# Batch 0 of a sketched attention with exact-GELU MLP on one Trainium2 core: 64x64 products against 128x128 products with block-diagonal operands

## The chip, the cores and the metric

The kernel runs on one core of one Trainium2 chip. The metric is the device time in microseconds (us) of one execution; three runs of the kernel before took 259.84, 259.01 and 259.58 us, median 259.58. A core has five engines that run side by side and wait for each other by semaphores: PE (TensorE, matrix products, with its weight loads shown apart as PEld), DVE (VectorE), ACT (ScalarE), POOL (GpSimd) and SP (which here only issues DMAs). Each works through its own instructions in the order of the program.

## The reference

Attention with polynomial-sketch features, and behind it a two-layer MLP. Inputs: q, k, v of shape 4 batches x 4 heads x 1088 tokens x 32, two sketch matrices S1, S2 of 8 x 32, w_in 128 x 2048 and w_out 2048 x 128.

```python
def phi(x):                                  # 64 features of a token
    a = einsum('rd,bhsd->bhsr', S1, x)
    b = einsum('rd,bhsd->bhsr', S2, x)
    return einsum('bhsi,bhsj->bhsij', a, b)  # flattened to 64
kv  = einsum('bhsf,bhsd->bhfd', phi(k), v)
z   = sum(phi(k), over tokens)
num = einsum('bhsf,bhfd->bhsd', phi(q), kv)
den = einsum('bhsf,bhf->bhs', phi(q), z) + 1e-6
x   = num / den                              # heads side by side: 4352 x 128
out = gelu_exact(x @ w_in) @ w_out
```

## The kernel before, in words

Everything is float32. A batch has 1024 main tokens and 64 remaining ones; the main tokens of a batch are two chunks of 512 columns, so there are eight main chunks (n = 0 to 7) and a ninth of all remainders. An added dependency keeps every engine to the order of the program's text.

**Batch 0 starts the kernel** and is built differently from the rest, because the MLP can't begin before its first chunk of x is there. Its steps, in the order of the text:

- Keys are turned on PE (`key_turn` and `key_turn_apart`, lines 341 and 369). `kT[r]` then has on its 128 partitions four consecutive tokens x 32 channels of one head, and 512 columns: two heads (r and r+2) x two chunks x 128.
- `key_products` (L384, its matmul at L390) multiplies them by the sketches. The right operand S12 is 128 x 64 and block-diagonal, four blocks of 32 channels x 16 features. The kernel before uses only the two diagonal halves: for each 64 columns of kT and each half t of the partitions one 64x64 product with 32 columns of S12, 16 instructions for one r. Half t of the partitions goes to bank t.
- `key_features` (L395 on) copies one factor out of PSUM by ACT (L406, or all of it at L403) and multiplies the 64 features on DVE (L407), or for one of the four halves on POOL (L404).
- `expand_products` (L557, query side, chunk 0), then `kv_first` (L434) sums features times values over the tokens. `kv_first` picks the features of token i out of bank t and place as the key products left them.
- The remaining tokens follow (L416, L440), and ACT copies the sums, 2 x 33 columns (32 of kv, one of z) on 2 x 64 partitions, into `kz[0]` (L941).
- `numerators_by_token` (L670): for chunk 0 and 1 the numerators and denominators with the tokens on the partitions. Per token group of 128, per r, per half of 64 tokens and per head pair c one 64x64 product with 33 columns: 8 instructions per group. Chunk 0 goes in two parts of two groups into two banks each; chunk 1 takes four groups at once.
- `expand_products(1)` (L557 again) stands behind chunk 0's numerators on PE.
- `divide` adds 1e-6 to the denominators (L687; for the second part ACT does it, `denominators`, L701), takes the reciprocal (L688) and multiplies (L693), one DVE operation of 128x128 per bank and half.
- The quotients are turned back (L716, L708), copied to xT (L717, L710), and `first_hidden` (L751) and `hidden` (L735) start the MLP; `project` (L872) is its second layer for the first chunks.

Chunk 1's numerators are called at step t == 3 of the MLP loop (L1188), between `hidden` (L735) and `project` (L872). Later batches use other code (L445, L592, L647, L989), and the later MLP blocks a scheme with seven products in place of eight (L821); the change touches neither. At step 40 `repeat_first_z` (L506) takes batch 0's kv and z once more out of `kz[0]` for the remaining tokens.

The PSUM banks come from three rings of two: `hidden_bank` (h_ps), `out_bank` (o_ps) and `work_banks` (w_ps, two banks each).

Of the kernel before, what the change touches and what calls it, by code (L numbers as in the profile page):

```python
# [8 lines left out]
FP = mybir.dt.float32  # L9
U32 = mybir.dt.uint32  # L10
AX = mybir.AluOpType
ACT = mybir.ActivationFunctionType
# [4 lines left out]
def kernel(  # L17
# [18 lines left out]
    pe, dve, act, pool, sp = nc.tensor, nc.vector, nc.scalar, nc.gpsimd, nc.sync  # L36
    B, H, S, D = q.shape
    R = S1.shape[0]
    F = R * R
# [3 lines left out]
    NP = H // 2  # L43
    J = S // 128
    MAIN = J * 128
    REM = S - MAIN
    JC = 4
    CW = JC * 128
    G = 128 // 32
    NCH = J // JC  # L50
    C = D + 1
# [8 lines left out]
    big = ctx.enter_context(tc.tile_pool(name="big", bufs=1))  # L60
# [13 lines left out]
    def halves(banks):  # L74
        return [banks[:, i] for i in range(2)]

    def hidden_bank():
        return hps.tile([128, CW], FP, name="h_ps")

    def out_bank():  # L80
        return ops.tile([128, CW], FP, name="o_ps")
# [149 lines left out]
    kz = [big.tile([128, 128], FP, name=f"kz{b}") for b in range(B)]  # L231

    kz_first = big.tile([128, 128], FP, name="kz_first")

    ones = big.tile([128, D], FP, name="ones")

# [1 line left out]
    pool.memset(v_rem_aug[0], 0.0)  # L238
    pool.memset(v_rem_aug[0][:REM], 1.0)
    dve.memset(ones, 1.0)  # L240

    v_aug = [att.tile([128, NP, J, 2 * D], FP, name="sums") for r in range(2)]
    for t in v_aug:
# [78 lines left out]
    S12 = big.tile([128, H, 2 * R], FP, name="S12")  # L322
# [58 lines left out]
        return dict(out=out, in0=a[:, :, :, None].broadcast_to([128, n, R, R]),  # L381
                    in1=b[:, :, None, :].broadcast_to([128, n, R, R]))

    def key_products(r, banks, col=0):  # L384

        for i in range(2 * NCH):
            for c in range(2):
                for t in range(2):
                    at = i * 128 + c * 64
                    pe.matmul(banks[t][c * 64:(c + 1) * 64, col + i * 32:col + (i + 1) * 32],  # L390
                              lhsT=kT[r][t * 64:(t + 1) * 64, at:at + 64],
                              rhs=S12[t * 64:(t + 1) * 64, 2 * t:2 * t + 2].rearrange("p h r -> p (h r)"),
                              start=True, stop=True)

    def key_features(b, r, banks, by_pool=()):  # L395
        key_products(r, banks)
# [28 lines left out]
    def flat(features):  # L425
        return features.rearrange("p i j -> p (i j)")

    def kv_first(ps, r, tokens=range(J)):

        for i in tokens:  # L430

            ch, t, one = i // 4, i // 2 % 2, i % 2
            for c in range(NP):
                pe.matmul(ps[c * F:(c + 1) * F, r * 2 * D:r * 2 * D + C], lhsT=flat(k_p[0, r][:, t, c * 4 + ch * 2 + one]),  # L434
                          rhs=v_aug[r][:, c, i, :C], start=(r == 0 and i == 0), stop=False, skip_group_check=True)

    def kv_first_rem(ps):
# [67 lines left out]

    def repeat_first_z():  # L506

        of = kz[0].rearrange("f (r x) -> f r x", r=2)
        to = kz_first.rearrange("f (c r d) -> f c r d", c=NP, r=2)
        for c in range(NP):  # L510
            act.copy(out=to[:F, c], in_=of[c * F:(c + 1) * F, :, 0:D])
        zs = att.tile([128, 2, D], FP, name="z_cols")
        pool.tensor_copy(out=zs, in_=of[:, :, D:C].broadcast_to([128, 2, D]))
        held["zs"] = zs

    def turn_first_kv():
# [142 lines left out]

    x_tok = {}  # L660

    def numerators_by_token(n, banks, tokens):

        for at, i in enumerate(tokens):
            for r in range(2):
                for half in range(2):
                    for c in range(NP):
                        rows, col, tok = slice(c * F, (c + 1) * F), (at * 2 + r) * C, i * 128 + half * 64
                        v_at = r * 2 * D
                        pe.matmul(banks[c][half * 64:(half + 1) * 64, col:col + C], lhsT=qp[n][rows, r, tok:tok + 64],  # L670
                                  rhs=kz[0][rows, v_at:v_at + C], start=True, stop=True)

    def x_half(n, i):
        x_tok[n, i] = att.tile([128, 2, H, D], FP, name=f"x_tok{i}", bufs=1)
        return x_tok[n, i]

    def divide(n, banks, tokens, by_head_pair, den=None):

        g = len(tokens) * 2
        given = den is not None  # L680
        if not given:
            den = att.tile([128, NP, JC * 2], FP, name="den_tok")[:, :, :g]
        parts = [slice(c, c + 1) for c in range(NP)] if by_head_pair else [slice(0, NP)]
        nd = [(banks[c.start][:, None] if by_head_pair else banks)[:, :, :g * C].rearrange("p b (g c) -> p b g c", c=C)
              for c in parts]
        for c, x in zip(parts, nd) if not given else ():
            dve.tensor_scalar(out=den[:, c], in0=x[:, :, :, D], scalar1=1e-6, scalar2=None, op0=AX.add)  # L687
        dve.reciprocal(out=den, in_=den)  # L688
        for i in range(len(tokens) // 2):
            to = x_half(n, tokens[0] // 2 + i).rearrange("p j (c r) d -> p c j r d", c=NP)  # L690
            for c, x in zip(parts, nd):
                for b in range(c.stop - c.start):
                    dve.tensor_mul(out=to[:, c.start + b], in0=x[:, b, i * 4:i * 4 + 4, 0:D].rearrange("p (j r) d -> p j r d", r=2),  # L693
                                   in1=den[:, c.start + b, i * 4:i * 4 + 4].rearrange("p (j r) -> p j r", r=2)[:, :, :, None]
                                   .broadcast_to([128, 2, 2, D]))

    def denominators(banks):

        den = att.tile([128, NP, JC * 2], FP, name="den_tok")[:, :, :JC]
        for c, ps in enumerate(banks):  # L700
            act.activation(out=den[:, c], in_=ps[:, :JC * C].rearrange("p (g c) -> p g c", c=C)[:, :, D], func=ACT.Copy, bias=1e-6)  # L701
        return den

    def turn_half_apart(n, i, banks):
# [220 lines left out]
    for i in range(2):  # L925
        query_features(0, i)
    kv_bank = out_bank()
    kv_first(kv_bank, 0, (0, 1, 4, 5))
    key_turn_rem(0, banks[1], by_act)
    kv_first(kv_bank, 0, (2, 3, 6, 7))  # L930
    key_features_rem(0, banks[1])
    kv_first(kv_bank, 1)
    kv_first_rem(kv_bank)
# [3 lines left out]
    w_in[0].exponents()  # L937
    late = []
    query_turn(1, lambda **a: late.append(a))
    kz_of, kv_of = (x.rearrange("f (r x) -> f r x", r=2)[:, :, :C] for x in (kz[0], kv_bank[:, :128]))  # L940
    act.copy(out=kz_of, in_=kv_of)  # L941
    w_in[0].mantissas()
    w_in[0].signs()
    w_in[0].product(pool)
# [3 lines left out]
    by_act(**late[0])  # L948
    w_in[1].low_words()
    parts = [range(2), range(2, JC)]  # L950
    nd = [[hidden_bank(), hidden_bank()], [out_bank(), out_bank()]]
    for banks, tokens in zip(nd, parts):
        numerators_by_token(0, banks, tokens)
    den = denominators(nd[1])
    expand_products(1)
    divide(0, nd[0], parts[0], by_head_pair=True)
    w_in[1].exponent_fields()
    w_in[1].exponents()
    divide(0, nd[1], parts[1], by_head_pair=True, den=den)
    turn_half(0, 0, hidden_bank(), by_act)  # L960
    w_in[1].mantissa_fields()
    turn_half_apart(0, 1, [out_bank(), out_bank()])
# [212 lines left out]
    for t in range(len(steps) + LAG):  # L1175
        if t < 4:

            hidden(0, t)
            if t == 1:
                w_out[0].low_words()  # L1180
                w_out[0].exponents()
                w_out[0].finish()
                w_out[1].fields()
            if t == 2:
                w_out[1].low_words()
            if t == 3:
                banks = work_banks()
                numerators_by_token(1, halves(banks), range(JC))  # L1188
                w_out[1].mantissas(by_pool=True)
                w_out[1].exponents()  # L1190
                divide(1, banks, range(JC), by_head_pair=False)
                w_out[1].signs()
                w_out[1].product()
                project(0, 0)
                project(0, 1, cols=slice(0, 256))
                turn_half(1, 0, work_bank(), by_act)
                project(0, 1, cols=slice(256, 512))
                turn_half(1, 1, work_bank(), by_dve)
            continue
        if t == 4:  # L1200
            first_hidden(1, 0)
            for f, *a in products[t]:
                f(*a)
            first_hidden(1, 1)
        for n in drains[t]:
            drain(n)
        sooner = t == NMAIN * NF
        if sooner:
            for f, *a in products[t]:
                f(*a)  # L1210
        if t < len(steps):
            n, fi = steps[t]
            hidden(n, fi, by_halves=t >= 18 and (n < NMAIN or fi < 5))
        if t < len(steps) and steps[t][0] < NMAIN and steps[t][1] % NB == NB - 1:
            n, b = steps[t][0], steps[t][1] // NB
            if b >= first_block(n):
                token_sums(n, b)
        for f in slots[t]:
            f()
        for n in done[t]:  # L1220
            store(n)
        if t != 4 and not sooner:
            for f, *a in products[t]:
                f(*a)
# [41 lines left out]
```

## Time and profile before

| what | value |
|---|---|
| median of three runs | 259.58 us (259.01 to 259.84) |
| the profiled execution's own time | 259.29 us |
| its span, first to last instruction | 257.5 us (1.8 us lie around it) |
| PE busy | 253.3 us, 98% |
| weight loads (PEld) | 135.0 us, 52% |
| DVE busy | 151.7 us, 59% |
| ACT busy | 114.4 us, 44% |
| POOL busy | 164.1 us, 64% |
| mean granted TensorE clock | 1.0 |

A float32 matrix product appears in the trace as two records, and so does its weight load; a transpose by PE is one record of each. So "x32" beside a group of products means 16 instructions. Shapes such as 64*64 are the rows and columns of the array that the product uses; the shape behind it is that of the moving operand. A record's duration includes the way through the array, so products that follow each other overlap in the list: the pace is read from start to start. A product whose weights are not in yet is recorded early and with a longer duration.

### The profile page before, as it was taken

How to read it: one execution, taken by the hardware profiler on the slowest of the kernel's cores; microseconds unless marked ns; L12 is line 12 of the kernel's file. 1: busy time of each engine (PE TensorE's matmuls, PEld its weight loads, DVE VectorE, ACT ScalarE, POOL GpSimd, SP SyncE). 2: the span in 40 equal slices, each digit the busy share in tenths (PEclk: the TensorE clock that was granted, in tenths of full speed). 3: DMA queues.
4: the chain of work that ended last, by engine and by line, in shares of the span. 5: the costliest groups of instructions: out<-in, count | busy, mean ns of one | idle time of the engine just before them, and what ended most of it. 6: DMA issues, size and time to landing. Idle time of an engine off the chain costs nothing.

```text
span 257.5 us, 5763 instructions
## 1 busy us (share of the span) xinstructions
PE 253.3 (98%) x2333; PEld 135.0 (52%) x2333; DVE 151.7 (59%) x317; ACT 114.4 (44%) x221; POOL 164.1 (64%) x173
## 2 busy tenths in 40 slices
PE   8999999999999999999999999999999999999995
PEld 6856444355444545444444455455544444445794
DVE  3886879969698987580178976399307000700330
ACT  3685767433635333533335332523444334433442
POOL 3503016799968788587758775787758777877300
PEclk9999999999999999999999999999999999999999
DMA  6479848820000101101000002000200200020020
GB/s 208 136 221 368 179 105 210 224 47 10 3 0 13 30 1 23 20 12 31 3 0 3 0 10 36 1 1 3 41 3 7 37 0 1 7 36 0 3 41 20
DMA packets 29082, 13.48 MB, mean 52 GB/s; under 512 B 21888, under 2 KB 27264, under 8 KB 29056
## 3 DMA queue, kind: packets, MB, share of 16 engines
q1 hardware_dynamic: 28624, 12.79, 20.2%
q8 instruction: 18, 0.29, 0.5%
q10 hardware_dynamic: 432, 0.33, 0.4%
q14 instruction: 8, 0.07, 0.1%
HBM read 10.88 MB, written 2.23 MB: 51 GB/s over the span
## 4 chain that ended last, share of the span: by engine, by line
PE 98%; DVE 1%; issue 0%; ACT 0%; DVEq 0%
PE h_ps L735 45%; PE o_ps L821 33%; PE o_ps L872 5%; PE w_ps L869 3%; PE w_ps L445 1%; PE w_ps L592 1%; PE w_ps L904 1%; PE w_ps L647 1%; PE o_ps L434 1%; PE h_ps L751 1%; PE w_ps L989 1%; PE w_ps L557 0%; PE w_ps L670 0%; DVE x_tok L693 0%; PE h_ps L341 0%; PE w_ps L341 0%
## 5 line engine op out<-in xcount | busy, mean ns | idle before, releaser
L735 PE MATMUL h_ps<-xT,w_in 128*64 128x512 f32 (+3 forms) x514 | 136.8, 576 | 0.0
L742 ACT ACTIVATE block<-h_ps 128x512 f32<-128x512 f32 (+1 forms) x128 | 73.0, 571 | 117.3 <-PE h_ps L735 115.3
L735 PEld LDWEIGHTS h_ps<-xT,w_in 128*64 128x64 f32 (+1 forms) x514 | 41.7, 142 | 30.6 <-issue 11.9
L821 PE MATMUL o_ps<-block,w_out 128*64 128x256 f32 x224 | 57.5, 379 | 0.0
L786 POOL TENSOR_TENSOR bits_low<-block 128x512 f32<-128x512 f32 x28 | 36.1, 1290 | 27.6 <-ACT block L742 27.6
L821 PEld LDWEIGHTS o_ps<-block,w_out 128*64 128x64 f32 x224 | 30.5, 137 | 38.1 <-issue 27.6
L787 POOL TENSOR_TENSOR bits_a<-block 128x512 f32<-128x512 f32 x28 | 35.7, 1276 | 11.8 <-ACT block L742 11.6
L836 DVE COPY sums<-o_ps 64x256 f32<-64x256 f32 x8 | 3.3, 417 | 60.6 <-PE o_ps L821 60.6
L789 POOL TENSOR_TENSOR bits_m<-block,bits_e 128x512 f32<-128x512 f32 x28 | 36.0, 1287 | 2.2
L788 POOL TENSOR_TENSOR bits_e<-bits_a,block 128x512 f32<-128x512 f32 x28 | 36.0, 1286 | 2.2
L821 PE MATMUL o_ps<-block,small 128*64 128x256 f32 x112 | 28.8, 379 | 0.0
L821 PE MATMUL o_ps<-bits_a,small 128*64 128x256 f32 x112 | 28.8, 379 | 0.0
L821 PE MATMUL o_ps<-bits_low,small 128*64 128x256 f32 x112 | 28.8, 379 | 0.0
L821 PE MATMUL o_ps<-bits_m,w_out 128*64 128x256 f32 x112 | 28.7, 379 | 0.0
L821 PEld LDWEIGHTS o_ps<-block,small 128*64 128x64 f32 x112 | 15.2, 137 | 17.9 <-issue 10.8
L821 PE MATMUL o_ps<-bits_e,small 128*64 128x256 f32 x112 | 17.0, 383 | 0.0
L872 PE MATMUL o_ps<-g,w_out 128*128 128x512 f32 (+1 forms) x34 | 16.5, 572 | 0.0
L821 PEld LDWEIGHTS o_ps<-bits_m,w_out 128*64 128x64 f32 x112 | 15.3, 137 | 0.0
L821 PEld LDWEIGHTS o_ps<-bits_a,small 128*64 128x64 f32 x112 | 15.2, 137 | 0.0
L821 PEld LDWEIGHTS o_ps<-bits_low,small 128*64 128x64 f32 x112 | 15.2, 137 | 0.0
L604 DVE STREAM_TRANSPOSE w_ps<-w_ps 128x512 f32<-128x512 f32 (+1 forms) x7 | 4.8, 687 | 17.1 <-ACT xT L658 12.7
L821 PEld LDWEIGHTS o_ps<-bits_e,small 128*64 128x64 f32 x112 | 7.6, 137 | 10.6 <-issue 8.8
(197 smaller groups left out, 303.3 us busy)
## 6 DMA issues: line engine op xcount, KB each, us to landing
block<-in_moe_w_in_dram SPq DMA_DIRECT2D x3, 512.0 KB, 9.9
block<-in_moe_w_out_dram SPq DMA_DIRECT2D x3, 512.0 KB, 10.4
k<-in_k_dram SPq DMA_DIRECT2D x12, 128.0 KB, 2.8
v<-in_v_dram SPq DMA_DIRECT2D x12, 128.0 KB, 3.1
q<-in_q_dram SPq DMA_DIRECT2D x24, 64.0 KB, 2.6
out_dram<-oT SPq DMA_DIRECT2D x21, 64.0 KB, 2.2
q_first<-in_q_dram SPq DMA_DIRECT2D x2, 256.0 KB, 3.9
v<-in_v_dram SPq DMA_DIRECT2D x2, 256.0 KB, 4.5
```

Source lines behind the costliest of these rows:

```text
L434: pe.matmul(ps[c * F:(c + 1) * F, r * 2 * D:r * 2 * D + C], lhsT=flat(k_p[0, r][:, t, c * 4 + ch * 2 + one]), rhs=v_aug[r][:, c, i, :C], s ...
L604: dve.transpose(out=tok, in_=ps[:, :, :H2])
L735: pe.matmul(ps[rows, :W], lhsT=w[:, rows], rhs=xT[n][:, :W], start=True, stop=True)
L742: act.activation(out=g_of[n, fi][:, :W], in_=ps[:, :W], func=ACT.Gelu)
L786: pool.tensor_sub(out=s[3], in0=a11, in1=a21)
L787: pool.tensor_add(out=s[1], in0=a21, in1=a22)
L788: pool.tensor_sub(out=s[2], in0=s[1], in1=a11)
L789: pool.tensor_sub(out=s[4], in0=a12, in1=s[2])
L821: pe.matmul(acc[n][bank][half * 64:(half + 1) * 64, col:col + HW], lhsT=fixed, rhs=moving, start=opens and e == 0 and name in "4715", stop ...
L836: dve.tensor_copy(out=N[lo, 0, one], in_=a0[lo, one])
L869: pe.matmul(o_of[n][i][:, :128], lhsT=g[:, i * 128:(i + 1) * 128], rhs=w_tile(w_out_sb, fi), start=first, stop=final)
L872: pe.matmul(o_of[n][:, cols], lhsT=w_tile(w_out_sb, fi), rhs=g[:, cols], start=first, stop=final)
```

## The change

Three edits, all of them in batch 0.

1. `key_products` uses the whole block-diagonal S12: one product of 128 rows and 128 columns with 64 moving columns for each 128 columns of kT, 4 instructions for one r instead of 16. Bank c now holds chunk c and not half t; `kv_first` looks its features up accordingly and is called for tokens 0 to 3 and 4 to 7 (before: 0, 1, 4, 5 and 2, 3, 6, 7).
2. A new tile `kz_apart` (128 x 2 x 2 x 33) is set to zero at the start by DVE. ACT copies the sums into its diagonal blocks, in two copies of 64 partitions instead of one of 128. `numerators_by_token` then takes 128 tokens, both head pairs and both halves in one product of 128 rows and columns with 66 moving columns: 2 instructions per token group instead of 8. Two token groups fit one bank, so each part of chunk 0 uses one bank instead of two.
3. `divide` handles a bank at a time: one addition, one reciprocal over all given banks, and one multiplication of 128x256 per bank, where two of 128x128 stood before. `denominators` is one ACT operation instead of two.

```diff
+    kz_apart = big.tile([128, 2, NP, C], FP, name="kz_apart")
+    dve.memset(kz_apart, 0.0)
...
-        for i in range(2 * NCH):
-            for c in range(2):
-                for t in range(2):
-                    at = i * 128 + c * 64
-                    pe.matmul(banks[t][c * 64:(c + 1) * 64, col + i * 32:col + (i + 1) * 32],
-                              lhsT=kT[r][t * 64:(t + 1) * 64, at:at + 64],
-                              rhs=S12[t * 64:(t + 1) * 64, 2 * t:2 * t + 2].rearrange("p h r -> p (h r)"),
-                              start=True, stop=True)
+        for c in range(NCH):
+            for x in range(2):
+                at = (x * NCH + c) * 128
+                pe.matmul(banks[c][:, x * 64:(x + 1) * 64], lhsT=kT[r][:, at:at + 128],
+                          rhs=S12.rearrange("p h r -> p (h r)"), start=True, stop=True)
...
-            ch, t, one = i // 4, i // 2 % 2, i % 2
-                pe.matmul(ps[...], lhsT=flat(k_p[0, r][:, t, c * 4 + ch * 2 + one]),
+                pe.matmul(ps[...], lhsT=flat(k_p[0, r][:, i // JC, c * JC + i % JC]),
...
-            act.copy(out=to[:F, c], in_=of[c * F:(c + 1) * F, :, 0:D])
+            act.copy(out=to[:F, c], in_=kz_apart[c * F:(c + 1) * F, :, c, 0:D])
-        pool.tensor_copy(out=zs, in_=of[:, :, D:C].broadcast_to([128, 2, D]))
+        for c in range(NP):
+            rows = slice(c * F, (c + 1) * F)
+            pool.tensor_copy(out=zs[rows], in_=kz_apart[rows, :, c, D:C].broadcast_to([F, 2, D]))
...
+            to = by_head(banks[at // 2]).rearrange("p (j c r) x -> p j r c x", j=2, c=NP)[:, at % 2]
             for r in range(2):
-                for half in range(2):
-                    for c in range(NP):
-                        rows, col, tok = slice(c * F, (c + 1) * F), (at * 2 + r) * C, i * 128 + half * 64
-                        v_at = r * 2 * D
-                        pe.matmul(banks[c][half * 64:(half + 1) * 64, col:col + C], lhsT=qp[n][rows, r, tok:tok + 64],
-                                  rhs=kz[0][rows, v_at:v_at + C], start=True, stop=True)
+                pe.matmul(to[:, r], lhsT=qp[n][:, r, i * 128:(i + 1) * 128], rhs=kz_apart[:, r], start=True, stop=True)
...
+            den = att.tile([128, NP, 2 * H], FP, name="den_tok")
+            for i, bank in enumerate(banks):
+                dve.tensor_scalar(out=den[:, i], in0=by_head(bank)[:, :, D], scalar1=1e-6, scalar2=None, op0=AX.add)
+        den = den[:, :len(banks)]
         dve.reciprocal(out=den, in_=den)
+        for i, bank in enumerate(banks):
+            dve.tensor_mul(out=x_half(n, first + i).rearrange("p j h d -> p (j h) d"), in0=by_head(bank)[:, :, 0:D],
+                           in1=den[:, i, :, None].broadcast_to([128, 2 * H, D]))
...
-    act.copy(out=kz_of, in_=kv_of)
+    for c in range(NP):
+        rows = slice(c * F, (c + 1) * F)
+        act.copy(out=kz_apart[rows, :, c], in_=kv_bank[rows, :128].rearrange("f (r x) -> f r x", r=2)[:, :, :C])
-    nd = [[hidden_bank(), hidden_bank()], [out_bank(), out_bank()]]
+    nd = [hidden_bank(), out_bank()]
```

More of the change, by code (lines that the diff above doesn't have):

```diff
@@ L382, in spread, with key_products @@
                     in1=b[:, :, None, :].broadcast_to([128, n, R, R]))
-    def key_products(r, banks, col=0):
-        for i in range(2 * NCH):
-            for c in range(2):
-                for t in range(2):
-                    at = i * 128 + c * 64
-                    pe.matmul(banks[t][c * 64:(c + 1) * 64, col + i * 32:col + (i + 1) * 32],
-                              lhsT=kT[r][t * 64:(t + 1) * 64, at:at + 64],
-                              rhs=S12[t * 64:(t + 1) * 64, 2 * t:2 * t + 2].rearrange("p h r -> p (h r)"),
-                              start=True, stop=True)
+    def key_products(r, banks):
+        for c in range(NCH):
[3 more added lines that the diff above has]
+                          rhs=S12.rearrange("p h r -> p (h r)"), start=True, stop=True)
     def key_features(b, r, banks, by_pool=()):
@@ L430, in kv_first @@
         for i in tokens:
-            ch, t, one = i // 4, i // 2 % 2, i % 2
             for c in range(NP):
-                pe.matmul(ps[c * F:(c + 1) * F, r * 2 * D:r * 2 * D + C], lhsT=flat(k_p[0, r][:, t, c * 4 + ch * 2 + one]),
+                pe.matmul(ps[c * F:(c + 1) * F, r * 2 * D:r * 2 * D + C], lhsT=flat(k_p[0, r][:, i // JC, c * JC + i % JC]),
                           rhs=v_aug[r][:, c, i, :C], start=(r == 0 and i == 0), stop=False, skip_group_check=True)
@@ L506, in repeat_first_z @@
     def repeat_first_z():
-        of = kz[0].rearrange("f (r x) -> f r x", r=2)
         to = kz_first.rearrange("f (c r d) -> f c r d", c=NP, r=2)
         for c in range(NP):
-            act.copy(out=to[:F, c], in_=of[c * F:(c + 1) * F, :, 0:D])
+            act.copy(out=to[:F, c], in_=kz_apart[c * F:(c + 1) * F, :, c, 0:D])
         zs = att.tile([128, 2, D], FP, name="z_cols")
-        pool.tensor_copy(out=zs, in_=of[:, :, D:C].broadcast_to([128, 2, D]))
+        for c in range(NP):
+            rows = slice(c * F, (c + 1) * F)
+            pool.tensor_copy(out=zs[rows], in_=kz_apart[rows, :, c, D:C].broadcast_to([F, 2, D]))
         held["zs"] = zs
@@ L660, with by_head @@
     x_tok = {}
+    def by_head(bank):
+        return bank[:, :2 * H * C].rearrange("p (n x) -> p n x", x=C)
     def numerators_by_token(n, banks, tokens):
         for at, i in enumerate(tokens):
+            to = by_head(banks[at // 2]).rearrange("p (j c r) x -> p j r c x", j=2, c=NP)[:, at % 2]
             for r in range(2):
-                for half in range(2):
-                    for c in range(NP):
-                        rows, col, tok = slice(c * F, (c + 1) * F), (at * 2 + r) * C, i * 128 + half * 64
-                        v_at = r * 2 * D
-                        pe.matmul(banks[c][half * 64:(half + 1) * 64, col:col + C], lhsT=qp[n][rows, r, tok:tok + 64],
-                                  rhs=kz[0][rows, v_at:v_at + C], start=True, stop=True)
+                pe.matmul(to[:, r], lhsT=qp[n][:, r, i * 128:(i + 1) * 128], rhs=kz_apart[:, r], start=True, stop=True)
     def x_half(n, i):
@@ L675, in x_half, with divide, denominators @@
         return x_tok[n, i]
[L677 to L687, printed above, removed]
-        dve.reciprocal(out=den, in_=den)
[L689 to L701, printed above, removed]
+    def divide(n, banks, first, den=None):
+        if den is None:
+            den = att.tile([128, NP, 2 * H], FP, name="den_tok")
+            for i, bank in enumerate(banks):
+                dve.tensor_scalar(out=den[:, i], in0=by_head(bank)[:, :, D], scalar1=1e-6, scalar2=None, op0=AX.add)
+        den = den[:, :len(banks)]
+        dve.reciprocal(out=den, in_=den)
+        for i, bank in enumerate(banks):
+            dve.tensor_mul(out=x_half(n, first + i).rearrange("p j h d -> p (j h) d"), in0=by_head(bank)[:, :, 0:D],
+                           in1=den[:, i, :, None].broadcast_to([128, 2 * H, D]))
+    def denominators(bank):
+        den = att.tile([128, NP, 2 * H], FP, name="den_tok")
+        act.activation(out=den[:, 0], in_=by_head(bank)[:, :, D], func=ACT.Copy, bias=1e-6)
         return den
@@ L927 @@
     kv_bank = out_bank()
-    kv_first(kv_bank, 0, (0, 1, 4, 5))
+    kv_first(kv_bank, 0, range(JC))
     key_turn_rem(0, banks[1], by_act)
-    kv_first(kv_bank, 0, (2, 3, 6, 7))
+    kv_first(kv_bank, 0, range(JC, J))
     key_features_rem(0, banks[1])
@@ L939 @@
     query_turn(1, lambda **a: late.append(a))
-    kz_of, kv_of = (x.rearrange("f (r x) -> f r x", r=2)[:, :, :C] for x in (kz[0], kv_bank[:, :128]))
-    act.copy(out=kz_of, in_=kv_of)
+    for c in range(NP):
+        rows = slice(c * F, (c + 1) * F)
+        act.copy(out=kz_apart[rows, :, c], in_=kv_bank[rows, :128].rearrange("f (r x) -> f r x", r=2)[:, :, :C])
     w_in[0].mantissas()
@@ L950 @@
     parts = [range(2), range(2, JC)]
-    nd = [[hidden_bank(), hidden_bank()], [out_bank(), out_bank()]]
-    for banks, tokens in zip(nd, parts):
-        numerators_by_token(0, banks, tokens)
+    nd = [hidden_bank(), out_bank()]
+    for bank, tokens in zip(nd, parts):
+        numerators_by_token(0, [bank], tokens)
     den = denominators(nd[1])
     expand_products(1)
-    divide(0, nd[0], parts[0], by_head_pair=True)
+    divide(0, nd[:1], 0)
     w_in[1].exponent_fields()
     w_in[1].exponents()
-    divide(0, nd[1], parts[1], by_head_pair=True, den=den)
+    divide(0, nd[1:], 1, den)
     turn_half(0, 0, hidden_bank(), by_act)
@@ L1190 @@
                 w_out[1].exponents()
-                divide(1, banks, range(JC), by_head_pair=False)
+                divide(1, halves(banks), 0)
                 w_out[1].signs()
```

## Prediction

> **What bounds the kernel now.** I read the page's chain first, then the chain in order of time for the first 25 us, then the timelines of the stages that the change touches.
>
> ```profile
> PE 98%; DVE 1%; issue 0%; ACT 0%; DVEq 0%
> ```
>
> The end is set by PE. In order of time (start us, us, what):
>
> ```profile
> 6.00 0.60 PE o_ps L390 x32
> 6.60 0.47 PE h_ps L390 x32
> 7.07 1.25 PE w_ps L557 x28
> ...
> 11.81 0.67 PE h_ps L670 x32
> 12.48 0.22 DVE den_tok L687 x2
> ```
>
> The reader is to see that every product the change replaces (L390, L670) stands on this chain, and that of VectorE's quotients a few pieces do, near 12.5 to 14.4 us. From 25 us on the busy time of PE equals the length of the stretch (35.00 of 35.00 us, 180.00 of 180.00 us in the table by stretches): nothing later gives back what the start loses, and nothing there waits for a transfer. So the question is how many us later PE reaches the MLP.
>
> **What the products cost.** A float32 product is two records. From the timelines around 6 and 15 us:
>
> ```profile
> 5.93 0.56 PEld L390 LDWEIGHTS o_ps<-S,kT 64*64 64x64 f32 x32 [0.17 <-ACT kT L343]
> 6.39 0.56 PEld L390 LDWEIGHTS h_ps<-S,kT 64*64 64x64 f32 x32
> ...
> 14.82 0.97 PEld L751 LDWEIGHTS h_ps<-xT,w_in 128*128 128x128 f32 x8
> ```
>
> The second group of 32 loads starts 0.46 us behind the first: four records, one on each quarter of the array, cost 0.058 us together, 0.0146 us each. In L751, with 128 rows and columns, 8 loads start within 0.97 - 0.19 (the last one's own duration) = 0.78 us, 0.111 us apart, with products of 128 columns beside them. The form that the change makes, 128*128 with 64 moving columns, is in the trace once:
>
> ```profile
> 46.02 0.33 PE L416 MATMUL w_ps<-S,kT_rem 128*128 128x64 f32 x2
> 46.03 0.19 PEld L416 LDWEIGHTS w_ps<-S,kT_rem 128*128 128x128 f32 x1 [0.24 <-issue]
> 46.14 0.30 PEld L872 LDWEIGHTS o_ps<-g,w_out 128*128 128x128 f32 x2
> ```
>
> Its two products start 0.33 - 0.275 = 0.055 us apart (0.275 is the longest of the two in the line's list), but loads of 128 columns still start 0.11 us apart (46.03, 46.14, and 46.14 + 0.30 - 0.19 = 46.25). So a record costs 0.110 us by its load, and the product hides beside the next load. Bounds: 0.055 us, were the products alone to set the pace, and 0.166 us, were load and product to follow each other. I take 0.110, which two rows of the same form give. A new record then does the work of four old ones (0.058 us) in 0.110: the block-diagonal operand loads no column less, and the four quarters no longer load side by side. [...]
>
> **Switching between array shapes** costs too:
>
> ```profile
> 18.06 0.59 PE L735 MATMUL h_ps<-xT,w_in 128*128 128x512 f32 x1
> 18.58 1.14 PE L670 MATMUL w_ps<-kz,q_pT 64*64 64x33 f32 x64
> 19.65 0.70 PE L872 MATMUL o_ps<-g,w_out 128*128 128x512 f32 x1
> ```
>
> L735's products follow each other every 0.43 us, so L670 could have started at 18.49 and started 0.09 later. L872's first product lasts 0.70 instead of 0.59, so it really ran from 19.76. The change takes such switches away where 128*128 work stands next to the new products.
>
> **Part by part.**
>
> *Key products (2 x 16 records instead of 2 x 32).* Before: from 5.93 to about 6.89, and L557 starts at 7.00. After: 5.93 + 16 x 0.110 + 0.05 (last product) + 0.09 (switch) = 7.83, so +0.83. But L557 before lost time waiting for qT, which DVE turns until 7.14: from L557's start to L434's it took 8.25 - 7.00 = 1.25 us, and the same work later 13.86 - 12.81 = 1.05. After, qT is long there: -0.20. **+0.63.** Behind it: the first bank of r = 0 is complete slightly earlier than before; the copies for r = 1 start near 7.95 instead of 7.16 and POOL's features end near 9.3 instead of 8.9. They are needed by the kv products of r = 1, which PE reaches at 9.8 + 0.6, and POOL's second copy of values ends by 9.9: covered. A_sb, k_p_rem and L440 move with PE.
>
> *The copy into kz_apart.* Two ACT copies; L406's two of the same kind start 0.11 apart, so the second ends 0.1 us later than the one before did. Before, the first numerator came 0.16 us behind the copy (11.38 + 0.20 to 11.74), since PE had also to switch from the transposes; now it has not. I take **0.0** (-0.1 to +0.1). The memset falls into DVE's idle time before 2.3 us.
>
> *Numerators of chunk 0 (16 records instead of 64).* Before, from 11.74 to L557's start at 12.81: 1.07. After: 0.11 (first load) + 15 x 0.110 + 0.05 + 0.09 = 1.90. **+0.83.** L557 and the transposes L716 stand behind it on PE. VectorE has the first half's numerators (8 records) 0.3 us later than the shift so far, and still ends at about 14.3, a microsecond before PE reaches L716 at 13.86 + 1.46 = 15.32. The second half: numerators out at 14.3, ACT 0.2, reciprocal 0.2, a wait 0.24 as before, and one multiplication of 128x256 at 0.42 (as L421 takes) end at 15.3; PE comes to L708 at about 15.6. So **VectorE leaves the path; its own saving** (two times 0.49 us becomes two times 0.42, and one small operation less) **is worth 0**, hidden under PE's longer products. Were that cover gone, it would be worth up to 0.2 us. ACT's copy L717 then releases L751 with the same lag as before.
>
> *Numerators of chunk 1 (16 records instead of 64).* Before, 18.49 to 19.76: 1.27. After: no switch, the first load lies beside L735, 16 x 0.110 = 1.76. **+0.49.** The quotients take DVE about as long as before (two additions and two multiplications for one and four); they end about 0.15 us before PE needs them at L716, and w_out's rounding behind them 0.1 us before L872. Were this cover gone it would cost 0.1 to 0.3 us.
>
> *ACT and POOL at step 40*: one more POOL copy, beside PE work with 45 us to its use: 0. PSUM banks: fewer are taken, and each was released long before.
>
> **Sum**: 0.63 + 0.0 + 0.83 + 0.49 = +1.95 us. The profiled execution took 259.29 us (span 257.5 and 1.8 around it), which gives 261.24; from the median of the three runs, 0.29 higher, 261.53. I forecast 261.4, **slower by 0.7%**.
>
> **Rivals.**
>
> *Faster: PE's pace is set by the number of records.* 48 records instead of 192 at the old average of 0.0146 us would take 0.70 us instead of 2.80. The key products' part would be lost to the wait for qT; the two parts of numerators would give 0.7 each and two switches 0.1: 259.3 - 1.5 = 257.8. It decides if a product of 128x128 with 64 columns costs no more than one of 64x64. [...] Against it: records on different quarters start 0.007 us apart in this trace, and L751 and L416 show 0.11 for the 128-wide ones. 5%.
>
> *No change: the new records run at their products' pace*, 0.055 us: 48 x 0.055 = 2.64 against 2.80, and the switches: 259.3 - 0.4 = 258.9. Against it stand the loads of L416, 0.11 apart. 4%.
>
> *Half of it: the early growth is covered*, because L434's start at 8.25 was set by POOL's copy of the values (the trace names it as releaser, but the copy had ended at 7.84) and not by PE: 261.4 - 0.6 = 260.8. 5%.
>
> *Slower still: loads and products of the new form don't overlap*, 0.166 us: 48 x 0.056 = 2.7 more, 264.1. Against it: L751's loads, 0.111 apart beside products of the same length. 4%.
>
> The forecast itself, with DVE's small margins and the scatter of the runs (259.0 to 259.8), 82%: 260.4 to 262.3. That is already 8 in 10, and the half case lies in it, so the range is 260.3 to 262.4.
>
> A measurement of this kernel can tell about 0.3%, 0.8 us, from no change. Faster by more: 0.05; within: 0.06; slower by more: 0.89.
>
> **What would show it.** In the profile after: L390's and L670's weight loads 128*128 at 0.11 us apart; L557 first at 7.8 and then at 14.3; L716 at 15.3; L872 effectively at 21.7 instead of 19.76; the same busy time of PE behind it, and the span 259.4 or so. Loads 0.055 apart, or L716 waiting for DVE, would make it wrong.

## The result, and the profile after

The changed kernel takes 261.58 us (median of six runs, 261.44 to 261.90) against 259.74 for the kernel before beside it: a ratio of 1.0076, with a 95% interval of 1.0062 to 1.0089, which is 2.0 us slower. The forecast was 261.4, range 260.3 to 262.4. A second set of runs on another occasion (after_again, below) gave 1.0080, 1.0055 to 1.0105.

The profiled execution took 261.90 us, span 260.1. Its chain, by engine:

```profile
PE 98%; ACT 0%; issue 0%
```

DVE, 1% before, is gone from the chain. In order of time (start us, us, what), the pieces that stand for those shown of before; L391 are the key products, L670 the numerators, L556 expand_products:

```profile
6.62 0.84 PE o_ps L391 x8
7.46 0.89 PE h_ps L391 x8
8.35 1.05 PE w_ps L556 x32
...
12.94 1.11 PE h_ps L670 x8
14.05 0.89 PE o_ps L670 x8
14.94 1.05 PE w_ps L556 x32
...
20.72 1.73 PE w_ps L670 x16
```

Chunk 1's numerators before, in the same view:

```profile
18.65 1.07 PE w_ps L670 x64
```

A quarter of the records, and each group longer: 0.89 us where 32 quarter-array records took 0.47, 1.73 where 64 took 1.07. L556 takes 1.05 us both times: its wait for qT is gone. The loads of these products (timeline, PEld):

```profile
7.24 0.97 PEld L391 LDWEIGHTS h_ps<-S,kT 128*128 128x128 f32 x8
...
13.83 0.97 PEld L670 LDWEIGHTS o_ps<-kz_apart,q_pT 128*128 128x128 f32 x8
...
20.56 1.75 PEld L670 LDWEIGHTS w_ps<-kz_apart,q_pT 128*128 128x128 f32 x15 [0.24 <-issue]
```

Eight loads in 0.97 us with 0.19 for the last one: 0.111 us from start to start, as in L751 before. VectorE's part (timeline, DVE; the first line is of before, the others of after):

```profile
12.97 0.49 DVE L693 TENSOR_TENSOR x_tok<-h_ps,den_tok 128x128 f32<-128x128 f32 x2
```

```profile
14.09 0.17 DVE L681 TENSOR_SCALAR den_tok<-h_ps 128x8 f32<-128x8 f32 x1 [1.06 <-PE h_ps L670]
...
14.52 0.42 DVE L685 TENSOR_TENSOR x_tok<-h_ps,den_tok 128x256 f32<-128x256 f32 x1
...
15.50 0.42 DVE L685 TENSOR_TENSOR x_tok<-o_ps,den_tok 128x256 f32<-128x256 f32 x1
```

0.42 us for a half, where two operations of 128x128 took 0.49; but it first waits 1.06 us for PE, and the first half's quotients end at 14.94, a microsecond before PE turns them at 15.92.

The way from the first key product to the first product of `project` (L872 before), step by step, as starts of PE's records (us), in the kernels that the rest of the text uses. The first product of `project` is recorded early (it lasts 0.65 to 0.70 us instead of 0.59), so its start is taken 0.43 us, the pace of these products, ahead of the second one's. The last row ends at the start of PE's last record:

| from ... to | before | after | after_again | keys_only | nums_only | column_halves |
|---|---|---|---|---|---|---|
| first key product, at | 5.93 | 6.43 | 5.46 | 5.84 | 6.20 | 6.38 |
| key products to L557 | 1.06 | 1.85 | 1.93 | 1.93 | 1.06 | 1.08 |
| L557 to the kv products | 1.25 | 1.05 | 1.05 | 1.05 | 1.25 | 1.23 |
| kv products to the transposes of q | 2.91 | 2.93 | 2.93 | 2.93 | 2.92 | 2.92 |
| those to the numerators | 0.58 | 0.68 | 0.68 | 0.58 | 0.68 | 0.68 |
| numerators to L557 again | 1.07 | 1.93 | 1.93 | 1.07 | 1.93 | 1.09 |
| L557 to the quotients' transposes | 1.05 | 1.05 | 1.05 | 1.05 | 1.05 | 1.05 |
| those to the MLP, L751 | 0.99 | 0.99 | 0.99 | 0.99 | 0.99 | 0.99 |
| L751 to chunk 1's numerators | 3.73 | 3.64 | 3.64 | 3.73 | 3.64 | 3.73 |
| those to `project` | 1.17 | 1.79 | 1.79 | 1.17 | 1.79 | 1.19 |
| key products to `project`, in all | 13.82 | 15.91 | 15.99 | 14.50 | 15.31 | 13.96 |
| `project` to PE's last record | 234.30 | 234.31 | 234.31 | 234.30 | 235.54 | 235.80 |

So the change costs 2.1 to 2.2 us in front of `project` and nothing behind it. The two profiled spans differ by 2.6: the remaining 0.5 us lie in front of the first changed instruction. Before and after, from the chains (transposes of the keys; lines 369 and 371 are the same code):

```profile
5.42 0.37 PE h_ps L369 x2
5.79 0.22 PE w_ps L369 x2
```

```profile
5.59 0.62 PE h_ps L371 x2
6.21 0.41 PE w_ps L371 x2
```

The same transposes, 0.11 us apart in the one execution and 0.21 in the other. That belongs to the execution and not to the kernel: in after_again's profile, of the same kernel, they run 0.11 us apart and the first key product starts at 5.46. These two executions of the changed kernel differ by 0.97 us in that start and by 0.91 us in their whole time (261.90 and 260.99). This is the reason to compare stretches and not whole spans.

The last two columns hold something that the forecast did not have: two kernels lose 1.2 and 1.5 us more, 135 us behind the last line that they change.

### The profile page after: what moved, and what is told of

Same layout as the page of the kernel before. It is cut to its first block, busy times and chain, and to the rows that moved or that the text cites. A ratio compares the mean times of both kernels' runs of the same rounds, so it can differ in the third digit from the quotient of the medians.

```text
span 260.1 us, 5471 instructions
## 1 busy us (share of the span) xinstructions
PE 255.8 (98%) x2189; PEld 137.9 (53%) x2189; DVE 151.7 (58%) x314; ACT 114.6 (44%) x221; POOL 163.9 (63%) x174
## 4 chain that ended last, share of the span: by engine, by line
PE 98%; ACT 0%; issue 0%
PE h_ps L725 45%; PE o_ps L811 33%; PE o_ps L862 5%; PE w_ps L859 3%; PE w_ps L443 1%; PE w_ps L591 1%; PE w_ps L894 1%; PE w_ps L646 1%; PE w_ps L556 1%; PE o_ps L432 1%; PE h_ps L741 1%; PE w_ps L670 1%; PE w_ps L980 1%; PE h_ps L670 0%; PE h_ps L343 0%; PE o_ps L670 0%
## 5 line engine op out<-in xcount | busy, mean ns | idle before, releaser
L725 PE MATMUL h_ps<-xT,w_in 128*64 128x512 f32 (+3 forms) x514 | 136.9, 576 | 0.0
L725 PEld LDWEIGHTS h_ps<-xT,w_in 128*64 128x64 f32 (+1 forms) x514 | 41.8, 142 | 30.5 <-issue 11.6
```

The source lines that it names most:

```text
L725: pe.matmul(ps[rows, :W], lhsT=w[:, rows], rhs=xT[n][:, :W], start=True, stop=True)
```

## The experiments

**1. keys_only**: the kernel before with the changed `key_products` and `kv_first` alone.

> The key products over 128 rows and columns alone; numerators and quotients as before. Load theory (a record costs 0.11 us per 128 columns of weights, four quarter-array records 0.058 us together): L557 starts about 0.8 us later and wins back its 0.2 us of waiting for qT, so 0.6 us slower than before (0.4 to 0.8). Rival 'half of it' (the early growth is covered because POOL's copy of the values sets L434's start): no change (0.0 to 0.2), and the numerators carry all of the change.

Measured: ratio 1.0017 (1.0006 to 1.0028), 0.44 us slower, inside the expected 0.4 to 0.8; from the key products to `project` 14.50 us, +0.68. As the load theory has it: +0.87 to L557, -0.20 behind it. L434's start moves with PE, so POOL's copy doesn't hold it, and the rival "half of it" falls.

**2. nums_only**: the changed kernel with `key_products`, `kv_first` and its calls of before.

> The numerators over 128 rows and columns and the quotients of a half in one operation; key products as before. Load theory: 0.1 for the copy into kz_apart, 0.85 for chunk 0, 0.5 for chunk 1, VectorE's saving hidden: 1.4 us slower than before (1.2 to 1.7), and with keys_only it adds up to the whole change. Rival 'half of it': 1.9 us, the whole change.

Measured: 1.0101 (1.0085 to 1.0118), 2.6 us slower: a miss. The front does what was expected, +1.49, and with keys_only adds up to the whole (0.68 + 1.49 = 2.17; 2.09 and 2.17 measured). The other 1.24 us arise in one place near 157 us.

**3. column_halves**: the changed kernel with each of the products cut in two halves of 64 columns of weights.

```diff
-                pe.matmul(to[:, r], lhsT=qp[n][:, r, i * 128:(i + 1) * 128], rhs=kz_apart[:, r], start=True, stop=True)
+                for half in range(2):
+                    tok = i * 128 + half * 64
+                    pe.matmul(to[half * 64:(half + 1) * 64, r], lhsT=qp[n][:, r, tok:tok + 64], rhs=kz_apart[:, r],
+                              start=True, stop=True)
```

(and the same in `key_products`)

> The changed kernel, but each product over 128 rows and columns is cut into two over 128 rows and 64 columns of weights (tokens 0 to 63 and 64 to 127), so that the two loads go to the two halves of the array; block-diagonal operands, one bank for both head pairs and the quotients in one operation stay. Load theory: loads of 64 columns, two side by side, 0.058 us a pair, so 16 pairs for the keys and 32 for the numerators take what the kernel before took; PE's growth is gone, L557 starts at 7.0 and 12.9, and the time is that of before, plus 0.1 for the two copies, less what VectorE saves: -0.3 to +0.15 us against before. Rival 'a record that uses all 128 rows costs 0.11 us whatever it loads': 96 records instead of the changed kernel's 48, about 4 us slower than before.

Measured: 1.0051 (1.0033 to 1.0069), 1.3 us slower: a miss in the total, for the same reason as 2. The front settles the disputed point, though. Its loads (timeline, PEld):

```profile
6.84 0.56 PEld L392 LDWEIGHTS h_ps<-S,kT 128*64 128x64 f32 x16
...
12.76 0.55 PEld L674 LDWEIGHTS o_ps<-kz_apart,q_pT 128*64 128x64 f32 x16
```

Twice the records, in 0.56 us instead of 0.97. From the key products to `project` it takes 13.96 us, 0.14 more than before and 2.0 less than the changed kernel, with the same block-diagonal operands and the same rows. What costs is 128 columns of weights in one load; two loads of 64, on the two halves of the array, go side by side: they start 0.007 us apart (as L434's loads of this shape in before), and eight such pairs take 0.46 us (6.38 to 6.84), 0.058 each.

**4. halves_two_quotients**: column_halves with two operations of 128x128 for a half's quotients.

```diff
-            dve.tensor_mul(out=x_half(n, first + i).rearrange("p j h d -> p (j h) d"), in0=by_head(bank)[:, :, 0:D],
-                           in1=den[:, i, :, None].broadcast_to([128, 2 * H, D]))
+            to = x_half(n, first + i)
+            for j in range(2):
+                dve.tensor_mul(out=to[:, j], in0=by_head(bank)[:, j * H:(j + 1) * H, 0:D],
+                               in1=den[:, i, j * H:(j + 1) * H, None].broadcast_to([128, H, D]))
```

> column_halves with the quotients of a half in two operations of 128x128 instead of one of 128x256. With PE's growth gone, VectorE has no cover here. If VectorE's saving is on the path without cover, this is 0.1 to 0.2 us slower than column_halves; if the transposes L716 and ACT's copy set the start of the MLP anyway, it is the same within 0.1 us and the span in front of L751 doesn't move.

Measured: 1.0054 (1.0038 to 1.0071) against column_halves' 1.0051: the same. The trace shows 0.05 us: PE's transposes start 1.10 us behind L557 instead of 1.05. So without cover VectorE's saving is worth 0.05 us, a quarter of the 0.2 that was allowed for it.

**5. after_again**: the changed kernel.

> The changed kernel once more, as the base for the two that follow: 1.9 us slower than before (1.6 to 2.2). In its profile PE's transposes in front of the key products may run at either pace, since in the first profile of it they ran 0.21 us apart until 6.4 us, and in that of before only until 4.9 us; the first key product then starts between 5.9 and 6.5, and from there the steps are as in the first profile.

Measured: 1.0080 (1.0055 to 1.0105), 2.1 us; the steps of the first profile (table).

**6. two_quotients**: the changed kernel with the edit of 4.

> The changed kernel with the quotients of a half in two operations of 128x128 instead of one of 128x256 (the products stay over 128 rows and columns). If VectorE is off the path under PE's longer products, as forecast, the time is that of the changed kernel within 0.15 us (most of that from chunk 1, where the margin was 0.1 to 0.15 us). Rival 'VectorE's operations are on the path': 0.2 to 0.4 us slower than the changed kernel.

Measured: 1.0083 (1.0056 to 1.0111), and from the key products to `project` 15.99 us, as in after_again. Under PE's longer products VectorE's saving is worth nothing.

**7. wide_moving**: the changed kernel with the moving operand of the key products doubled.

```diff
-                pe.matmul(banks[c][:, x * 64:(x + 1) * 64], lhsT=kT[r][:, at:at + 128],
-                          rhs=S12.rearrange("p h r -> p (h r)"), start=True, stop=True)
+                to = banks[c].rearrange("p (k n) -> p k n", k=2)[:, :, x * 64:(x + 1) * 64]
+                pe.matmul(to, lhsT=kT[r][:, at:at + 128],
+                          rhs=S12.rearrange("p h r -> p (h r)")[:, None, :].broadcast_to([128, 2, 64]), start=True, stop=True)
```

> The changed kernel with the moving operand of the key products twice as wide: S12 is sent through twice, 128 columns instead of 64, and the second result goes to a part of the bank that nothing reads. Load theory: the records stay 0.11 us apart, as L751's with 128 columns, because the load and not the product sets the pace; the time is that of the changed kernel within 0.1 us. Rival 'the products' own length adds to the load's': 16 records by 0.055 us, 0.9 us slower than the changed kernel.

Measured: 1.0086 (1.0060 to 1.0112), 15.94 us from the key products to `project`. Its loads:

```profile
7.22 0.97 PEld L392 LDWEIGHTS h_ps<-S,kT 128*128 128x128 f32 x8
```

The same 0.97 us with 128 moving columns as with 64: the product hides wholly beside the next load. That the load sets the pace by itself shows in the profile after, where L725's products are 0.43 us apart and two loads of 128 columns still start 0.11 us apart (timeline, PEld; 0.30 less the last one's 0.19):

```profile
17.77 0.30 PEld L725 LDWEIGHTS h_ps<-xT,w_in 128*128 128x128 f32 x2
```

**The stop near 156 us.** In nums_only, column_halves and halves_two_quotients PE stands still in the middle of one group of small products, the query sketches of the last chunks. The chain of column_halves:

```profile
153.82 1.25 PE w_ps L445 x80
155.07 0.59 PE w_ps L648 x16
155.67 1.26 PE w_ps L593 x53
156.92 0.92 issue
157.84 0.62 PE w_ps L593 x4
```

"issue" is time in which the engine waited for nothing that the profile shows; and PE has no recorded wait for a semaphore in this group. But the page lists DMA queues of the kind "instruction", taken here for those that carry the program itself. One of them (queue, packets, MB, share; of before):

```profile
q8 instruction: 18, 0.29, 0.5%
```

18 packets of 16 KB. Counting PE's recorded instructions (products, loads and waits) at the starts of these packets gives 143 to 387 from one to the next, and 249 on average (254 in the profile after), so a packet is taken to be a block of some 250 instructions of PE, an estimate from these counts. The expectations below set it at 256, which the counts leave open and run 9 tests. The stop comes at the 3010th recorded instruction of PE in nums_only and column_halves and at the 3011th in halves_two_quotients, which has one recorded wait more; by products and loads alone it is the 2984th in all three. In each of them a block's packet arrives 1.4 to 1.5 us before PE goes on (156.33 and 157.84 in column_halves); what fills the time between the two is not shown. These three kernels have 192 products and loads fewer than the kernel before, keys_only has 96 fewer, the changed kernel 288: if the blocks are such, theirs end elsewhere in the program. Three more kernels test that.

**8 to 10. Padding.** The last of the four products that only keep PE busy at the start is replaced by small ones, 25 of 32x32 (24 instructions more, 96 records) or 17 of 32x45 (16 more, 64 records), while PE waits for the keys.

```diff
-    keep_busy(1, bank, 192)
+    for i in range(25):
+        noughts = [nc.const_aps.tensor(0.0, [128, m], FP) for m in (32, 32)]
+        g = i % 4
+        pe.matmul(bank[g * 32:(g + 1) * 32, CW - 32:], lhsT=noughts[0], rhs=noughts[1], start=True, stop=True)
```

> column_halves with the last of the four products that keep PE busy at the start (192 columns) replaced by 25 small ones of 32x32 on the four column groups: 24 instructions of PE more, 96 records, in a stretch where PE waits for keys anyway. Theory of the program's blocks: PE's program comes in loads of 16 KB, one for some 256 recorded instructions; in nums_only, column_halves and halves_two_quotients, each with 192 records less than before, PE stands still for 1.0 to 1.5 us near 156 us at the same 3010th recorded instruction, because a block ends there behind a dense run of small products and the next one lands late beside the store of a chunk. With 96 more records the blocks end where those of keys_only do, which had no such stop: the stop goes, 1.0 to 1.5 us less than column_halves, so 0.0 to +0.3 us against before. Rival: the stop belongs to the work itself (the later start shifts the store or VectorE against PE), then it stays and the time is that of column_halves, 1.3 us over before.

Measured: 1.0011 (1.0002 to 1.0020), 0.3 us over before instead of column_halves' 1.3. Its chain at the place of the stop:

```profile
153.75 1.25 PE w_ps L445 x80
155.00 0.59 PE w_ps L648 x16
155.60 1.30 PE w_ps L593 x57
156.90 0.58 PE o_ps L816 x4
```

No stop; from `project` to PE's last record 234.30 us, as before. The remaining 0.3: 0.15 in the front, and the padding makes PE turn the keys some 0.2 us later (4.49 instead of 4.27).

> The kernel before with the last of the four products that keep PE busy replaced by 17 small ones of 32x45: 16 instructions more, 64 records, so that the blocks of 256 end where those of nums_only do (192 less or 64 more is the same place). Theory of the program's blocks: nothing else changes, and PE stands still near 155 us for 0.8 to 1.5 us among the query sketches of the last chunks: 1.0 us slower than before (0.7 to 1.5). Rival 'the stop belongs to the changed work': no change, within 0.2 us.

Measured: 1.0051 (1.0033 to 1.0069), 1.3 us slower, although no line but the padding differs from the kernel before. Its chain:

```profile
154.99 1.22 PE w_ps L592 x52
156.21 0.41 issue
156.62 0.63 PE w_ps L592 x5
```

The stop is at the 3266th recorded instruction: 3010 + 256, as blocks of 256 would have it. In the trace it costs 0.96 us from `project` to the end (235.26 against 234.30); the padding's later turn of the keys (4.44 instead of 4.27) comes on top.

> nums_only with the same 24 instructions more as halves_padded. Theory of the program's blocks: the stop of 1.2 us near 157 us goes, and what is left is what the front shows, 1.5 us over before (1.2 to 1.8); then keys_only (0.7 at the front) and this add up to the changed kernel's 2.1. Rival: it stays at 2.6 us over before.

Measured: 1.0065 (1.0049 to 1.0080), 1.7 us instead of 2.6; no stop behind `project`. With keys_only's 0.44 it gives 2.1, the changed kernel's whole; some 0.2 us of the 1.7 will be the padding's own, as in 8, which the intervals cannot separate.

How many instructions of PE stand in front of this group decides the stop: shown by taking it away (8, 10) and by making it (9). It came with 192 records fewer than before and with 64 more, counts that differ by 256, and not with 0, 96 or 288 fewer. That fits the ends of PE's blocks, and the rival, that the stop belongs to the changed work, falls with 9. That the block comes late because the chunk's store is under way at that time (three to four DMAs of small packets from 152 to 157 us) was only argued: a run with the store elsewhere wasn't tried.

## Why the prediction was right, step by step

- **A record of 128 columns of weights costs 0.110 us, paced by its load**: right, 0.111 in every group but a first one that starts beside slow transposes (1.10 us in place of 0.97 in the first profile after; 0.111 in after_again). Neither bound (0.055 and 0.166) came true. The lower one was misread: L416's second product starts 0.055 us behind the first but lasts 0.275 us against 0.219, so it ends 0.11 us behind it, as far as the loads are apart; the sum did not use it, the rival "no change" did. wide_moving shows that the product's length doesn't count up to 128 columns (0.97 us for eight loads, as with 64), column_halves that loads of half the width bring the old pace back (0.058 us a pair).
- **Key products +0.83, of which 0.20 come back at L557**: +0.79 to +0.87 and -0.20. L557 starts with all of qT there, as forecast.
- **The copy into kz_apart 0.0 (-0.1 to +0.1)**: +0.10, the upper bound. The second copy was mis-sized: it starts 0.20 us behind the first, not 0.11, so the copying ends 0.21 us later. The first numerator comes 0.05 us behind it instead of 0.16, which gives 0.11 back; that this is the missing switch was not tested.
- **Numerators of chunk 0 +0.83**: +0.86. **Of chunk 1 +0.49**: -0.09 in front (no switch) and +0.62, together +0.53.
- **VectorE leaves the path, its saving is worth nothing**: right (two_quotients). The allowance of up to 0.2 without cover was too large: 0.05 (halves_two_quotients).
- **Nothing later gives anything back**: 234.31 against 234.30 us. Right, but by luck in one respect: the forecast took the program behind `project` as fixed, and never asked what 288 fewer instructions do to the loading of the program. Had it been 192 fewer, as in nums_only, another 1.2 us would have come on top.
- **The sum, 1.95**: 2.09 and 2.17 in the two traces, 2.0 and 2.1 by the runs. Each term was off by 0.03 to 0.10: the copy and the numerators came out longer, the key products 0.04 shorter in the first trace and 0.04 longer in the second. So the 1.95 came out by its mechanism, and the terms did not have to make up for each other.
- **Rivals**: the pace by number of records falls with column_halves, which has twice the changed kernel's records and is faster; in before, products that sit side by side in the array took 0.0146 us a record, four of them for one undivided record of 0.111. "No change" and "slower still" fall with the load's 0.111, "half of it" with keys_only.

## What to carry to other kernels

Here a block-diagonal operand saved instructions, not array time: count columns of weights per load and how many loads go side by side (0.111 us for a load of 128 columns, 0.058 for two of 64 or four on quarters). Where a float32 product moves fewer columns than it loads (here 64 and 66 against 128), try column halves (all rows, 64 columns each): here they kept one PSUM bank for both head pairs, as the full product does, at the pace of the small ones (1.08 and 1.09 us in the table, where those took 1.06 and 1.07). And when the number of instructions of the busiest engine changes, look along the whole chain for an "issue" piece that has appeared elsewhere, before the difference is put down to the edit.

## What the runs showed of the hardware that was not expected

- PE loses 0.96 to 1.50 us (0.4 to 0.9 as "issue" in the chain) at one place in a dense run of small products, and the number of its instructions ahead of it decides whether; 64 added records in the first 5 us move the stop in, 96 take it out, 150 us later. The end of a 16 KB block of the program fits as the cause.
- The pace of the first transposes of the keys, 0.11 or 0.21 us apart up to about 6.4 us, changes from execution to execution of one kernel and moves its front by up to 1 us (first key product at 6.43 and 5.46 in two profiles of the changed kernel). The traces' record of the granted clock starts, at full speed, at 6.5 us in the first of these profiles, at 4.1 in the second and at 5.0 in that of before. In the first and in that of before the pace changes about there: transposes start 0.21 us apart until 6.2 and 4.9 us, what follows 0.11 apart (the key loads from 6.6 us, the transposes from 5.5). In the second the transposes of the keys stand behind 4.1 and run 0.11 us apart. What sets that time, and that the clock sets the pace, was not shown.
